# Placing VectorE's products of x with sine and cosine where GpSimd is planned idle, with narrower filler matmuls and a newly searched order

## The chip, the cores and the metric

One core of one Trainium2 chip. The metric is the device time of one execution in microseconds. Each run also has a span (first to last instruction, some 1.8 us less than the time) and a mean granted TensorE clock, 1.00 being full speed. A run is called slow here when it is over 1.5% above the fastest run of its own kernel, otherwise fast.

## The reference

Two stages follow each other. The first is a linear attention with a decaying state, over 4 batches, 8 heads, 768 steps and head size 48. The second works on its output x of 4 x 768 x 384:

```python
theta = x @ w_theta
zr, zi = x * cos(theta), x * sin(theta)
y = einsum('ts,bsd->btd', w_tok_r, zr) + einsum('ts,bsd->btd', w_tok_i, zi)
u = x + y
return u + maximum(u @ w_ch, 0)
```

## The kernel before

The kernel cuts the sequence into 24 chunks of 128 steps. For each it records operations (an engine, a modelled duration, dependencies, buffers). A list scheduler in the kernel's own text then simulates the engines and puts all operations into one order, and they are issued in that order. Semaphores between engines follow only from data and buffers. This is the part that places one operation (`free_at` holds the planned end of each engine's last one):

```python
    def place(self, o, free_at):
        ...                                   # cut: buffers
        for i, (eng, dur, fn, pen) in enumerate(o.alts):
            t = max(free_at.get(eng, 0.0), t_slot)
            for d in o.deps:
                t = max(t, d.end + (LAG[d.eng] if d.eng != eng else 0.0))
            ...                               # cut: loads
            out.append((t + dur + pen, t, eng, dur, i))
        return out
```

Tables named SHIFT, PENALTY, SLACK and WIN bias that order. They were found by a search. Copies have alternatives on two engines (`alts`), and the planner picks one, so other tables also move copies between VectorE and ScalarE. The operations that the change is about, `z`, are the products of x with sine and cosine:

```python
    def phases(g, ahead):
        deps = [st[g[-1]]["o_xc"]]
        ...
        toS = P.op("ACT", 1.3, lambda: table("trig_and_small"), deps, mode="toS", ...)
        ...                                   # cut: theta on TensorE, then:
            o_s = P.op("ACT", ACT(384), f_s, [o_th, toS], [], [], mode="S", ...)   # sine
            o_c = P.op("ACT", 0.46, f_c, [o_s], [], [th], mode="S", ...)           # cosine
            def f_z(b=b, c=c, sc=sc):
                xb = x_all[:, b, c:c + 1, :].to_broadcast([L, 2, DM])
                nc.vector.tensor_tensor(get(zb[b])[:, c], xb, get(sc), op=ALU.mult)
            s["o_z"] = P.op("DVE", 0.69, f_z, [o_c, z_open[b]], ...)
        if g[-1] < NT - 1:
            P.op("ACT", 1.3, lambda: table("natural_log_exp_and_others"), cs, mode="toE", ...)
```

Filler matmuls on zeros were put in to keep TensorE's clock up; what this case shows of that is in e13 and e14 (with few of their columns three of six runs had a mean clock of 0.956, with more none was under 0.966). FLEAD = 33 of them stand ahead of everything, and later ones go into planned gaps, as many as the last 3.4 us of the plan lack of a target in columns. Each is counted as 128 columns:

```python
    wps = pads["cum"][0][:, 1, DM:]
    def fill():
        nc.tensor.matmul(wps, lhsT=warm[:, 0, :], rhs=warm[:, 1, :], start=True, stop=True)
```

## Time and profile before

| kernel before | |
|---|---|
| time, median of 3 runs (range) | 170.01 us (168.47 to 171.23) |
| span and clock of the profiled run | 168.1 us, 0.984 |
| TensorE without useful work (idle + fillers) | 25.7 of 168.1 us |
| useful TensorE time | 142.4 us |

"Useful" is the span less idle time and fillers. The prediction works this out by stretches.

From the page of the kernel before: each engine's busy time, share and instructions, and the granted clock in tenths over 40 equal slices of 4.2 us.

```profile
PE 153.9 (92%) x1986; PEld 103.7 (62%) x1986; DVE 132.3 (79%) x287; ACT 116.0 (69%) x264; POOL 112.4 (67%) x133
PEclk9959999999999999999999999999999999999997
```

TensorE is nearly always busy. The clock is at its top but for one slice, the third (and the very end). The first 5 us of the kernel before, the busy time of TensorE in the filler matmuls alone (columns: stretch, length, TensorE busy and count, weight loads, clock, DMA share, GB/s):

```profile
0.00:5.00 5.00, 3.88 (x36) 3.75 (x36) 1.00 0.56 137
```

Thirty-six fillers of 128 columns, 3.88 us, cover the time until the first input has come. At some 108 ns each they run at half the rate of later ones (four matmuls of as many columns later take 0.22 us, start to start), so the 1.00 that is printed for the clock before the first real work is not to be trusted. The lengths of single matmuls show when the half rate ends: at about 5.6 us here, 4.3 us in the changed kernel. Below this is called the first rise.

### The profile page before, as it was taken

To read this page: it belongs to the slowest core of one execution; us is meant where nothing else is said; L and a number is where in the kernel's file an instruction comes from. 1 tells how busy PE (TensorE), PEld (TensorE's weight loads), DVE (VectorE), ACT (ScalarE), POOL (GpSimd) and SP (SyncE) were. 2 spreads that over 40 slices of the span, in tenths; PEclk is the share of its full clock that TensorE was granted. 3 is DMA by queue.
4 is the path that set the end of the run, shared out by engine and by line. 5 is a ranking of instruction groups with operands and counts; after the bars stand their busy time and mean duration, and the time that the engine had idled before them with its cause. 6 is when DMAs were issued, how large, how long until landed. Compare 5 with 4: busy or idle time off the path is not lost.

```text
span 168.1 us, 5063 instructions
## 1 busy us (share of the span) xinstructions
PE 153.9 (92%) x1986; PEld 103.7 (62%) x1986; DVE 132.3 (79%) x287; ACT 116.0 (69%) x264; POOL 112.4 (67%) x133
## 2 busy tenths in 40 slices
PE   7997798995898999999999999999899999999981
PEld 7575476763665676657566677666566666666640
DVE  4506958899999988797899998899988997436361
ACT  3556585699889997667998696489979963932000
POOL 7198488997986689866367989999979921000000
PEclk9959999999999999999999999999999999999997
DMA  4999999897989999999999999897911101020312
GB/s 102 277 261 248 252 258 177 161 285 174 272 227 215 268 244 281 258 284 216 207 188 206 251 179 221 168 223 142 236 41 47 49 4 66 30 97 0 140 47 94
DMA packets 93769, 29.81 MB, mean 177 GB/s; under 512 B 88369, under 2 KB 92210, under 8 KB 93746
## 3 DMA queue, kind: packets, MB, share of 16 engines
q1 hardware_dynamic: 93344, 29.50, 79.2%
q8 instruction: 15, 0.25, 0.6%
q14 instruction: 8, 0.07, 0.2%
q10 hardware_dynamic: 402, 0.00, 0.1%
HBM read 24.78 MB, written 4.72 MB: 175 GB/s over the span
## 4 chain that ended last, share of the span: by engine, by line
PE 71%; DVE 11%; ACT 8%; POOL 3%; DMA 2%; issue 2%; ACTq 0%; POOLq 0%
PE bank L978 25%; PE bank L1005 7%; PE bank L941 4%; DVE sb_z L955 4%; PE cum L1073 3%; PE bank L611 3%; PE bank L548 3%; PE bank L992 2%; DMA in_w<-in_w_dram 2%; PE bank L606 2%; PE bank L530 2%; PE bank L532 2%; PE bank L632 2%; PE bank L1054 2%; PE cum L435 2%
## 5 line engine op out<-in xcount | busy, mean ns | idle before, releaser
L978 PE MATMUL bank<-sb_z,wtokT 128*128 128x384 bf16 x288 | 53.8, 326 | 0.0
L978 PEld LDWEIGHTS <-wtokT 128*128 128x128 bf16 x288 | 26.0, 98 | 14.9
L524 POOL TENSOR_TENSOR sb_bon<-sb_v,sb_rub 128x384 bf16<-128x384 bf16 x18 | 14.9, 829 | 13.5 <-DVE sb_rub L520 5.5
L955 DVE TENSOR_TENSOR sb_z<-x_all,sb_sc 128x768 bf16<-128x768 bf16 x24 | 20.2, 858 | 1.6 <-ACT sb_sc L949 1.6
L463 POOL TENSOR_TENSOR sb_q<-in_r,sb_a 128x384 bf16<-128x384 f32 x18 | 18.6, 1035 | 2.8 <-ACT sb_alt L449 2.4
L457 POOL TENSOR_TENSOR sb_k<-in_k,sb_a 128x384 bf16<-128x384 f32 x18 | 18.6, 1032 | 1.4 <-DMA in_k<-in_k_dram 1.4
L508 POOL TENSOR_TENSOR sb_ru<-in_r,u_bc 128x384 f32<-128x384 f32 x18 | 19.2, 1069 | 0.2
L987 DVE TENSOR_TENSOR sb_un<-bank,x_all 128x384 bf16<-128x384 f32 x24 | 13.3, 554 | 7.6 <-PE bank L978 7.3
L444 ACT ACTIVATE sb_a<-cum 128x768 f32<-128x768 f32 x18 | 14.8, 824 | 4.2 <-PE cum L439 2.7
L515 POOL TENSOR_TENSOR sb_ruk<-sb_ru,in_k 128x384 bf16<-128x384 f32 x16 | 17.2, 1075 | 0.5
L327 ACT ACT_TABLE_LOAD x12 | 15.4, 1283 | 1.5 <-PEq L1089 1.3
L1005 PE MATMUL bank<-wch,sb_uT 128*128 128x384 bf16 x72 | 15.5, 327 | 0.6 <-DVE sb_uT L999 0.5
L1010 DVE SCALAR_TENSOR_TENSOR sb_o<-bank,sb_un 128x384 f32<-128x384 f32 x24 | 13.2, 553 | 3.6 <-PE bank L1005 3.3
L1073 PE MATMUL cum<-warm 128*128 128x128 bf16 x106 | 11.6, 262 | 4.4 <-ACT sb_rub L783 1.8
L949 ACT ACTIVATE sb_sc<-bank,hpi 128x384 bf16<-128x384 f32 x24 | 14.7, 612 | 0.0
L941 PE MATMUL bank<-wth,sb_xT 128*128 128x384 bf16 x72 | 14.0, 326 | 0.3 <-ACT sb_sc L949 0.3
L536 DVE COPY sb_qkt<-bank 128x1024 bf16<-128x1024 bf16 x18 | 12.3, 684 | 1.6 <-PE bank L532 1.5
L946 ACT ACTIVATE sb_sc<-bank 128x384 bf16<-128x384 f32 x24 | 12.4, 516 | 1.4 <-PE bank L941 1.3
L996 ACT ACTIVATE sb_uT<-bank 128x384 bf16<-128x384 bf16 x14 | 7.0, 503 | 9.0 <-PE bank L992 8.9
L636 ACT ACTIVATE sb_xT<-bank 128x384 bf16<-128x384 bf16 x15 | 7.3, 496 | 8.3 <-PE bank L632 8.3
L553 DVE TENSOR_TENSOR sb_p<-bank,mask_exc 128x512 bf16<-128x512 f32 x18 | 12.3, 683 | 0.6 <-PE bank L548 0.5
L594 ACT ACTIVATE sb_S<-bank,sb_alt 128x48 bf16<-128x48 f32 x52 | 11.6, 323 | 1.7 <-PE bank L584 1.7
(135 smaller groups left out, 341.4 us busy)
## 6 DMA issues: line engine op xcount, KB each, us to landing
out_dram<-sb_o SPq DMA_DIRECT2D x24, 192.0 KB, 2.6
in_w<-in_w_dram SPq DMA_DIRECT2D x18, 192.0 KB, 4.9
in_r<-in_r_dram SPq DMA_DIRECT2D x18, 192.0 KB, 4.8
in_k<-in_k_dram SPq DMA_DIRECT2D x18, 192.0 KB, 4.5
in_v<-in_v_dram SPq DMA_DIRECT2D x18, 192.0 KB, 4.5
sb_w<-in_moe_w_tok_r_dram SPq DMA_DIRECT2D x6, 384.0 KB, 4.9
sb_w<-in_moe_w_tok_i_dram SPq DMA_DIRECT2D x6, 384.0 KB, 5.2
in_w<-in_w_dram SPq DMA_DIRECT2D x3, 384.0 KB, 5.0
```

Source lines behind the costliest of these rows:

```text
L327: nc.scalar.preload_act_table_set(name)
L444: nc.scalar.activation(get(a), get(cum)[:, :, :DM], AF.Exp)
L457: nc.gpsimd.tensor_tensor(get(kk)[:, :, :D], s["x_k"](), av(1), op=ALU.mult)
L463: nc.gpsimd.tensor_tensor(get(q)[:, :, :D], s["x_r"](), av(0), op=ALU.mult)
L508: nc.gpsimd.tensor_tensor(get(ru), s["x_r"](), u_bc, op=ALU.mult)
L515: nc.gpsimd.tensor_tensor(get(ruk), get(ru), s["x_k"](), op=ALU.mult)
L524: nc.gpsimd.tensor_tensor(get(bon), get(vb), get(rub).to_broadcast([L, H, D]), op=ALU.mult)
L941: nc.tensor.matmul(get(th), lhsT=get(s["xT"])[:, j, :], rhs=wth[:, j, :], start=(j == 0), stop=(j == NJ - 1))
L955: nc.vector.tensor_tensor(get(zb[b])[:, c], xb, get(sc), op=ALU.mult)
L978: nc.tensor.matmul(get(ac), lhsT=wtokT[:, q_, s_, ti, :], rhs=get(zb[b])[:, s_, q_, :], start=(s_ == 0 and q_ == 0), stop=(s_ == NCH - 1 a ...
L1005: nc.tensor.matmul(get(ml), lhsT=get(uT)[:, j, :], rhs=wch[:, j, :], start=(j == 0), stop=(j == NJ - 1))
L1073: nc.tensor.matmul(wps, lhsT=warm[:, 0, :], rhs=warm[:, 1, :], start=True, stop=True)
```

## The change

Intent: let the planner place each multiplication where VectorE and GpSimd are both free, because in the trace each takes longer beside the other (a multiplication took 0.56 us at 82.22 us, with GpSimd idle, and 1.20 at 83.68, with GpSimd at work, and GpSimd's next operation took 1.31 in place of 1.00); let it block GpSimd in the plan as well; and search the order anew with that. Nothing on the chip enforces the lock. With it come a dependency between table loads on ScalarE, which the planner needs to find an order at all, and fillers of 112 columns, clear of columns in which other results lie (H is 8). The planner still counts each filler as 128 columns.

```diff
+        self.lock = None
@@ place
             t = max(free_at.get(eng, 0.0), t_slot)
+            if o.lock:
+                t = max(t, free_at.get(o.lock, 0.0) - 0.02)
@@ order
                 free_at[eng] = o.end
+                if o.lock:
+                    free_at[o.lock] = max(free_at.get(o.lock, 0.0), o.end)
@@ the tables of the search (cut: two long lines)
-    SLACK = (3.98, 6.1)
+    SLACK = (3.34, 6.38)
-    WIN = {'PE': 0.1, 'ACT': 0.11, 'DVE': 0.16, 'POOL': 0.39, 'SP': 0.1}
+    WIN = {'PE': 0.0, 'ACT': 0.0, 'DVE': 0.11, 'POOL': 0.12, 'SP': 0.69}
@@ phases
+    modes = [None]
-        deps = [st[g[-1]]["o_xc"]]
+        deps = [st[g[-1]]["o_xc"], modes[-1]]
-            s["o_z"] = P.op("DVE", 0.69, f_z, ...)
+            s["o_z"] = P.op("DVE", 0.47, f_z, ...)
+            s["o_z"].lock = "POOL"
-            P.op("ACT", 1.3, lambda: table("natural_log_exp_and_others"), ...)
+            modes.append(P.op("ACT", 1.3, lambda: table("natural_log_exp_and_others"), ...))
@@ fillers
-    wps = pads["cum"][0][:, 1, DM:]
+    wps = pads["cum"][0][:, 1, DM + 2 * H:]
-        nc.tensor.matmul(wps, lhsT=warm[:, 0, :], rhs=warm[:, 1, :], start=True, stop=True)
+        nc.tensor.matmul(wps, lhsT=warm[:, 0, :], rhs=warm[:, 1, :L - 2 * H], start=True, stop=True)
```

More of the change, by code (lines that the diff above doesn't have):

```diff
@@ L212 @@
     OFF = {'ln': -2.2, 'cum': -2.1, 'exp': -2.05, 'alt': -2.04, 'q': -1.5, 'k': -1.45, 'v': -1.2, 'ru': -1.3, 'ruk': -1.2, 'rub': -1.2, 'bon': -1.1, 'tqk': -0.9, 'qkt': -0.9, 'p': -0.8, 'm0': -0.7, 'pc': -0.7, 'sel': -1.6, 'y': -0.5, 'x': -0.5, 'xt': -0.4, 'xc': -0.4, 'rk': -1.3, 'rkt': -1.2, 'rkc': -1.2, 'beta': -1.15}
-    SHIFT = {'M': -0.23, 'M@0': 3.78, 'M@1': -8.79, 'M@3': 4.37, 'Mp@0': 5.06, 'S': -3.32, 'S@0': 0.3, 'S@1': 4.4, 'S@3': -1.39, 'Sp@0': -0.82, 'alt': -2.71, 'alt@0': -6.46, 'alt@1': -5.24, 'alt@3': -1.0, 'bc@0': 2.73, 'beta@0': 6.96, 'bon': -7.28, 'bon@0': -11.25, 'bon@1': -1.68, 'bon@3': -15.43, 'cos': -4.6, 'cos@0': -8.64, 'cos@1': -3.05, 'cos@3': -4.08, 'cum': 2.98, 'cum@0': -0.21, 'cum@1': -0.34, 'cum@3': 0.03, 'cumo@0': -2.52, 'cump@0': 0.81, 'cwch': 2.19, 'cwch@1': 0.17, 'cwt': -0.63, 'cwt@1': -5.35, 'cwth': 0.26, 'cwth@1': -10.14, 'exk@0': 3.3, 'exp': -7.56, 'exp@0': -8.69, 'exp@1': -7.51, 'exp@3': -3.91, 'exq@0': -3.62, 'fin': 10.83, 'fin@0': 10.28, 'fin@1': 11.48, 'fin@3': 1.68, 'k': -2.66, 'k@0': -9.79, 'k@1': -1.84, 'k@3': 3.21, 'ldk': -0.07, 'ldk@0': 0.25, 'ldk@1': 0.18, 'ldk@3': -0.13, 'ldkp@0': -0.23, 'ldr': -0.52, 'ldr@0': -1.79, 'ldr@1': -1.7, 'ldr@3': -1.11, 'ldrp@0': -0.32, 'ldv': 0.27, 'ldv@0': 0.93, 'ldv@1': 0.57, 'ldv@3': 1.39, 'ldvp@0': 0.18, 'ldw': -1.63, 'ldw@0': -1.67, 'ldw@1': -2.55, 'ldw@3': -1.18, 'ldwp@0': -6.51, 'ln': -1.02, 'ln@0': 5.4, 'ln@1': -2.53, 'ln@3': 2.0, 'm': 1.57, 'm@0': 15.82, 'm@1': 14.98, 'm@3': 17.21, 'ml': 3.16, 'ml@0': -6.88, 'ml@1': -11.74, 'ml@3': -9.39, 'p': 4.22, 'p@0': 8.66, 'p@1': 17.51, 'p@3': 5.23, 'pc': 1.07, 'pc@0': 1.12, 'pc@1': -0.89, 'pc@3': -3.49, 'pp@0': -0.08, 'q': -0.33, 'q@0': -1.43, 'q@1': -1.77, 'q@3': 2.32, 'qkt': 1.93, 'qkt@0': 3.15, 'qkt@1': -5.42, 'qkt@3': -1.23, 'qktp@0': -4.05, 'rk@0': 4.47, 'rkc@0': 2.84, 'rkt@0': -3.15, 'ru': -2.75, 'ru@1': 3.2, 'ru@3': 4.03, 'rub': 1.54, 'rub@1': 3.87, 'rub@3': 6.62, 'ruk': -0.11, 'ruk@1': 4.75, 'ruk@3': 0.58, 'sel': 1.06, 'sel@0': 2.59, 'sel@1': 1.72, 'sel@3': -2.89, 'sin': 1.45, 'sin@0': 7.58, 'sin@1': 1.41, 'sin@3': 6.75, 'st': 0.43, 'st@0': -2.07, 'st@1': 5.27, 'st@3': -5.11, 'th': -5.14, 'th@0': -13.68, 'th@1': -11.99, 'th@3': -7.44, 'toE': -2.74, 'toE@0': 1.79, 'toE@1': 3.28, 'toE@3': 5.51, 'toS': -2.78, 'toS@0': 4.03, 'toS@1': 1.52, 'toS@3': 0.01, 'tok': -3.84, 'tok@0': -14.49, 'tok@1': -16.93, 'tok@3': -11.95, 'tqk': -0.37, 'tqk@0': -7.47, 'tqk@1': -3.98, 'tqk@3': -6.14, 'ubc': 3.86, 'ubc@1': -1.26, 'ublk@1': 12.81, 'ubm': 3.03, 'ubm@1': -0.13, 'uc': -4.81, 'uc@0': -0.8, 'uc@1': 1.76, 'uc@3': 5.44, 'un': 2.42, 'un@0': 3.41, 'un@1': 1.64, 'un@3': 0.26, 'ut': -3.32, 'ut@0': -11.88, 'ut@1': -17.65, 'ut@3': -16.65, 'v': 1.33, 'v@0': 1.16, 'v@1': 4.38, 'v@3': 2.97, 'wch': -0.56, 'wch@1': 4.47, 'wev': 2.67, 'wev@1': 3.64, 'wt': 0.86, 'wt@1': 1.37, 'wth': 0.4, 'wth@1': 0.12, 'wtr': 0.92, 'wtr@1': 4.43, 'x': 1.16, 'x@0': -4.58, 'x@1': -2.03, 'x@3': 1.47, 'xc': 1.62, 'xc@0': 0.36, 'xc@1': 6.08, 'xc@3': 2.79, 'xp@0': -4.33, 'xt': 0.48, 'xt@0': -1.77, 'xt@1': 4.35, 'xt@3': 2.35, 'y': -0.38, 'y@0': -2.78, 'y@1': 3.73, 'y@3': 5.0, 'yp@0': -0.46, 'z': -1.82, 'z@0': -4.98, 'z@1': -4.18, 'z@3': -2.79}
@@ L214 @@
-    PENALTY = {'S': 1.09, 'S@0': 1.12, 'S@1': -0.94, 'S@3': -3.96, 'bc@0': -0.71, 'bon@0': 2.38, 'cwch': -1.71, 'cwch@1': 2.81, 'cwt': 1.34, 'cwt@1': 3.16, 'cwth': 1.85, 'cwth@1': 0.93, 'k': 9.17, 'k@0': 10.47, 'k@1': 3.58, 'k@3': 6.59, 'pc': -1.22, 'pc@0': -2.79, 'pc@1': -4.91, 'pc@3': -5.2, 'qkt': 3.99, 'qkt@0': -0.11, 'qkt@1': 0.97, 'qkt@3': 1.62, 'qktp@0': 2.76, 'rk@0': 7.24, 'rkc@0': 3.74, 'ruk': -1.87, 'ruk@1': -0.54, 'ruk@3': -9.82, 'uc': 1.64, 'uc@0': -1.68, 'uc@1': 4.04, 'uc@3': -0.06, 'wev': -0.04, 'wev@1': -7.81, 'xc': -0.05, 'xc@0': -0.64, 'xc@1': 0.26, 'xc@3': 1.02, 'xp@0': 0.98}
+    SHIFT = {'M': -0.23, 'M@0': 3.78, 'M@1': -6.18, 'M@3': 6.62, 'Mp@0': 5.26, 'S': -3.32, 'S@0': 0.3, 'S@1': 6.59, 'S@3': 0.68, 'Sp@0': -0.68, 'alt': -2.71, 'alt@0': -7.92, 'alt@1': -3.85, 'alt@3': -3.16, 'bc@0': -2.41, 'beta@0': 8.1, 'bon': -7.28, 'bon@0': -11.68, 'bon@1': -4.82, 'bon@3': -16.83, 'cos': -4.6, 'cos@0': -10.9, 'cos@1': -3.18, 'cos@3': -6.72, 'cum': 2.98, 'cum@0': -0.21, 'cum@1': 0.55, 'cum@3': -3.61, 'cumo@0': -6.13, 'cump@0': 4.02, 'cwch': 2.19, 'cwch@1': -2.53, 'cwt': -0.63, 'cwt@1': -6.25, 'cwth': 0.26, 'cwth@1': -3.54, 'exk@0': 1.95, 'exp': -7.56, 'exp@0': -5.95, 'exp@1': -4.97, 'exp@3': -0.07, 'exq@0': -3.13, 'fin': 10.83, 'fin@0': 12.97, 'fin@1': 11.66, 'fin@3': 3.4, 'k': -2.66, 'k@0': -7.6, 'k@1': 3.92, 'k@3': 11.07, 'ldk': -0.07, 'ldk@0': 0.25, 'ldk@1': -0.41, 'ldk@3': -0.17, 'ldkp@0': 0.02, 'ldr': -0.52, 'ldr@0': -1.79, 'ldr@1': -1.92, 'ldr@3': -1.62, 'ldrp@0': -1.21, 'ldv': 0.27, 'ldv@0': 0.93, 'ldv@1': 0.19, 'ldv@3': 0.69, 'ldvp@0': 0.15, 'ldw': -1.63, 'ldw@0': -1.67, 'ldw@1': -2.09, 'ldw@3': -1.86, 'ldwp@0': -4.07, 'ln': -1.02, 'ln@0': 13.94, 'ln@1': 0.95, 'ln@3': 9.2, 'm': 1.57, 'm@0': 26.09, 'm@1': 23.77, 'm@3': 24.65, 'ml': 3.16, 'ml@0': -5.56, 'ml@1': -18.97, 'ml@3': -9.64, 'p': 4.22, 'p@0': 8.66, 'p@1': 14.97, 'p@3': 0.71, 'pc': 1.07, 'pc@0': 1.12, 'pc@1': -6.99, 'pc@3': -11.04, 'pp@0': -2.44, 'q': -0.33, 'q@0': -3.18, 'q@1': -3.3, 'q@3': -1.47, 'qkt': 1.93, 'qkt@0': 4.65, 'qkt@1': -1.14, 'qkt@3': -1.9, 'qktp@0': -2.73, 'rk@0': 3.64, 'rkc@0': 3.56, 'rkt@0': -3.48, 'ru': -2.75, 'ru@1': 3.01, 'ru@3': 2.84, 'rub': 1.54, 'rub@1': -1.69, 'rub@3': 6.59, 'ruk': -0.11, 'ruk@1': 3.88, 'ruk@3': 1.59, 'sel': 1.06, 'sel@0': 2.59, 'sel@1': -2.83, 'sel@3': -9.19, 'sin': 1.45, 'sin@0': 11.07, 'sin@1': 5.13, 'sin@3': 7.53, 'st': 0.43, 'st@0': -3.02, 'st@1': 2.87, 'st@3': -6.8, 'th': -5.14, 'th@0': -15.65, 'th@1': -4.15, 'th@3': -0.69, 'toE': -2.74, 'toE@0': -0.85, 'toE@1': -2.88, 'toE@3': 3.35, 'toS': -2.78, 'toS@0': 4.63, 'toS@1': 0.91, 'toS@3': 3.99, 'tok': -3.84, 'tok@0': -15.93, 'tok@1': -19.8, 'tok@3': -14.21, 'tqk': -0.37, 'tqk@0': -5.52, 'tqk@1': 1.97, 'tqk@3': -1.93, 'ubc': 3.86, 'ubc@1': -2.95, 'ublk@1': 19.95, 'ubm': 3.03, 'ubm@1': -2.04, 'uc': -4.81, 'uc@0': -6.32, 'uc@1': -4.14, 'uc@3': 1.48, 'un': 2.42, 'un@0': -1.4, 'un@1': -6.49, 'un@3': -9.41, 'ut': -3.32, 'ut@0': -10.56, 'ut@1': -21.29, 'ut@3': -18.71, 'v': 1.33, 'v@0': 4.75, 'v@1': 9.96, 'v@3': 8.06, 'wch': -0.56, 'wch@1': 4.81, 'wev': 2.67, 'wev@1': 3.84, 'wt': 0.86, 'wt@1': 1.04, 'wth': 0.4, 'wth@1': 0.61, 'wtr': 0.92, 'wtr@1': 6.87, 'x': 1.16, 'x@0': -4.58, 'x@1': -1.52, 'x@3': -1.66, 'xc': 1.62, 'xc@0': 4.23, 'xc@1': 7.28, 'xc@3': 6.11, 'xp@0': -7.19, 'xt': 0.48, 'xt@0': -10.11, 'xt@1': -2.37, 'xt@3': -3.74, 'y': -0.38, 'y@0': -2.78, 'y@1': 6.77, 'y@3': 10.43, 'yp@0': 0.4, 'z': -1.82, 'z@0': -5.82, 'z@1': -2.75, 'z@3': -3.52}
@@ new lines @@
+    PENALTY = {'S': 1.09, 'S@0': 1.12, 'S@1': -0.45, 'S@3': -2.12, 'bc@0': -0.34, 'bon@0': 0.28, 'cwch': -1.71, 'cwch@1': 3.73, 'cwt': 1.34, 'cwt@1': 1.4, 'cwth': 1.85, 'cwth@1': 1.11, 'k': 9.17, 'k@0': 12.79, 'k@1': 4.43, 'k@3': 8.94, 'pc': -1.22, 'pc@0': -2.79, 'pc@1': -2.21, 'pc@3': -2.5, 'qkt': 3.99, 'qkt@0': 2.63, 'qkt@1': 4.71, 'qkt@3': 4.28, 'qktp@0': 1.95, 'rk@0': 7.66, 'rkc@0': 1.91, 'ruk': -1.87, 'ruk@1': -1.25, 'ruk@3': -9.61, 'uc': 1.64, 'uc@0': -4.19, 'uc@1': 0.18, 'uc@3': -2.45, 'wev': -0.04, 'wev@1': -8.08, 'xc': -0.05, 'xc@0': -1.73, 'xc@1': -2.21, 'xc@3': 0.74, 'xp@0': -0.63}
@@ L955, in f_z @@
                 nc.vector.tensor_tensor(get(zb[b])[:, c], xb, get(sc), op=ALU.mult)
-            s["o_z"] = P.op("DVE", 0.69, f_z, [o_c, z_open[b]], [] if z_open[b] else [zb[b]], [sc], prio=g[-1] - 0.3, name=f"z{n}")
+            s["o_z"] = P.op("DVE", 0.47, f_z, [o_c, z_open[b]], [] if z_open[b] else [zb[b]], [sc], prio=g[-1] - 0.3, name=f"z{n}")
+            s["o_z"].lock = "POOL"
             z_open[b] = z_open[b] or s["o_z"]
@@ L959, in phases @@
         if g[-1] < NT - 1:
-            P.op("ACT", 1.3, lambda: table("natural_log_exp_and_others"), cs, mode="toE", prio=g[-1] - 0.3, name=f"toE{g[-1]}")
+            modes.append(P.op("ACT", 1.3, lambda: table("natural_log_exp_and_others"), cs, mode="toE", prio=g[-1] - 0.3, name=f"toE{g[-1]}"))
     def mixing(b, ti):
```

## The prediction

> **What bounds the kernel now.** I read four views of the kernel before, in this order: the engines' totals on the page, the busy time of every engine by stretch, the same table for the filler matmuls alone, and the order in time of VectorE and GpSimd around some of the multiplications that the change is about.
>
> The page's first part says that TensorE is busy for 92% of the span, VectorE for 79%, ScalarE 69%, GpSimd 67%. Averages over stages mislead, so the stretches come next. Columns: the stretch and its length, then busy us and instruction count of each engine, the granted clock, the DMA share and GB/s.
>
> ```profile
> 5.00:35.00 30.00, 26.11 (x488) 18.61 (x486) 19.52 (x48) 19.96 (x48) 22.78 (x26) 0.94 1.10 233
> 35.00:60.00 25.00, 21.05 (x319) 15.03 (x316) 24.21 (x46) 23.37 (x49) 20.52 (x21) 1.00 1.04 243
> 60.00:163.00 103.00, 102.01 (x1153) 65.89 (x1148) 85.03 (x169) 71.09 (x168) 65.35 (x68) 1.00 0.70 152
> ```
>
> From 60 to 163 us TensorE (first pair) is idle for only 103.00 - 102.01 = 1.0 us, so nothing that another engine saves there can shorten the span. From 35 to 60 us VectorE (third pair) is busy 24.21 of 25 us and ScalarE 23.37, while TensorE has idle time. TensorE's busy time also holds filler matmuls on zeros[...] (line 1073):
>
> ```profile
> 5.00:35.00 30.00, 5.13 (x52) 3.92 (x50) 0.94 1.10 233
> 35.00:60.00 25.00, 2.54 (x23) 1.50 (x20) 1.00 1.04 243
> ```
>
> TensorE's time without useful work is then: 5.0 us of start; 30.00 - 26.11 + 5.13 = 9.0 us up to 35 us; 25.00 - 21.05 + 2.54 = 6.5 us from 35 to 60; 1.0 us up to 163; and about 4.2 us of tail (0.89 busy of the last 5.10). Together 25.7 us; the other 142.4 of 168.1 us are useful TensorE work. The changed kernel must do the same useful work: the listing of its instructions differs on TensorE in fillers and order alone. So the change can only win from these 25.7 us, and really only from the 9.0 and the 6.5.
>
> The multiplication of x by sine and cosine is line 955, on VectorE, 24 times:
>
> ```profile
> L955 DVE TENSOR_TENSOR sb_z<-x_all,sb_sc 128x768 bf16<-128x768 bf16 x24 | 20.2, 858 | 1.6 <-ACT sb_sc L949 1.6
> L955 DVE TENSOR_TENSOR sb_z<-x_all,sb_sc x24: 543/840/1396, 38.1 to 148.6; 128x768 bf16<-128x768 bf16 x24
> ```
>
> One shape, yet 543 ns at the fastest, 840 at the median, 1396 at worst. The reason can be read off 82 to 86 us, VectorE first, then GpSimd (start, duration):
>
> ```profile
> 82.22 0.56 DVE L955 TENSOR_TENSOR sb_z<-x_all,sb_sc 128x768 bf16<-128x768 bf16 x1 [0.29 <-ACT sb_sc L949]
> 83.68 1.20 DVE L955 TENSOR_TENSOR sb_z<-x_all,sb_sc 128x768 bf16<-128x768 bf16 x1 [0.30 <-ACT sb_sc L949]
> ```
>
> ```profile
> 82.67 0.83 POOL L524 TENSOR_TENSOR sb_bon<-sb_v,sb_rub 128x384 bf16<-128x384 bf16 x1 [2.57 <-ACT sb_v L470]
> 83.46 1.00 POOL L515 TENSOR_TENSOR sb_ruk<-sb_ru,in_k 128x384 bf16<-128x384 f32 x1
> 84.41 1.31 POOL L457 TENSOR_TENSOR sb_k<-in_k,sb_a 128x384 bf16<-128x384 f32 x1
> ```
>
> At 82.22 GpSimd had nothing to do and the multiplication took 0.56 us. At 83.68 GpSimd was inside line 515 until 84.46; the multiplication ended at 84.88, some 0.42 us after it, and the next GpSimd operation took 1.31 us in place of 1.00. The two engines take turns, and both pay.
>
> [...]768 columns in 543 ns from SBUF, 384 in 554 ns from PSUM (line 987). [...]the granted clock is 1.00 everywhere from 15 us to 160 us.
>
> **The change, part by part.** The order is made by a list scheduler in the kernel's own text, with a modelled duration per operation; the changed tables are the outcome of a new search with it.
>
> 1. The multiplication is modelled at 0.47 in place of 0.69 us, may not start before GpSimd's running operation ends, and then holds GpSimd. No semaphore enforces it on the chip: only the order changes. In the trace the fast multiplication at 51.33 us gives way to the next VectorE instruction at 51.80, so 0.47 is its true step. Contention today costs VectorE 24 x (858 - 550) ns = 7.4 us, and GpSimd about 3.6 us (its four kinds of 1.00 us operation average 1.03 to 1.08). With real durations straying from the plan by a tenth or two, a multiplication that comes late meets the next GpSimd operation and waits a whole one. I therefore assume that only half is won: a mean of 0.70 us (estimate), 24 x 0.16 = 3.8 us of VectorE. Of these only the six between 35 and 60 us count (6.63 us busy today): 6.63 - 6 x 0.70 = 2.4 us.
> 2. Moved copies. The listing of instructions has six casts of x (548 ns) going from VectorE to ScalarE, ten copies to xT and seven to uT going from ScalarE (500 ns) to VectorE (350 ns), one copy of qkt (1.02 us) and two small ones also to VectorE, and one ruk product from VectorE (0.84) to GpSimd (1.07). Sum for VectorE: -7.2 if no multiplication waited at all, or -3.8 by my assumption, -3.3 + 3.5 + 2.5 + 1.1 + 0.4 - 0.8 = about -0.4 us; ScalarE: +3.1 - 5.0 - 3.5 - 1.0 - 0.4 = -6.8 us. But most xT and uT copies lie after 60 us, where TensorE sets the pace. In 35 to 60 us two casts (1.01 us together) leave VectorE for ScalarE. VectorE's load there falls by 2.4 + 1.0 = 3.4 us, to about 20.8 of 25; ScalarE's rises by 1.0 to 24.4 of 25 and takes its place. I take half of the 3.4, 1.7 us, as what TensorE gets back out of its 6.5.
> 3. Up to 35 us: the first twenty microseconds keep nearly the same order in the listing, and no engine is full (VectorE 19.52 of 30, GpSimd 22.78); this is latency of chains. Four casts leave VectorE. I allow 0.3 us.
> 4. Fillers: 113 of 112 columns in place of 106 of 128, and clear of the columns where beta lies. Waits of fillers for ScalarE's small copy sum to 1.8 us over five times before, but the listing still has a wait on fillers in ten places. I count nothing.
> 5. 60 to 163 us and the tail: useful work is the same, and both orders end alike (one last token product, then transpose, channel product, addition, store). Nothing.
>
> Sum: 1.7 + 0.3 = 2.0 us off the span of 168.1; off the time of 170.0 that gives 168.0.
>
> **The rivals.** (a) The lock is only on paper: order and jitter leave the multiplications at about 0.85 us, GpSimd's timetable slips by its reserved 24 x 0.47 = 11.3 us, and nothing is gained. For: [...]no semaphore between the two, and GpSimd is full in the stretch before 35 us. Against: GpSimd has nothing to do for over a quarter of the span. Time 169.5 to 170.5. (b) The early stage gets much better: with VectorE relieved, the token products (line 978), the large reserve of TensorE work, open earlier. For: in the new listing the first of them stands after about 29 us of useful TensorE work, in the old after about 32 ([...]an estimate from the listing and 0.162 us for 384 columns in the chain). Then half of the 15.5 us could shrink by a third: 165 to 166. Against: the new listing has more fillers before that point (109 against 106), a sign that the planner still expects gaps there. (c) VectorE becomes the bound between 60 and 140 us, where it is already at 85 to 97% and now gets seventeen more copies; if the multiplications still wait, TensorE loses 1 to 2 us: 170 to 171.5.
>
> **Range and chances.** The middle is 168.0. Rival (b) sets the low end at 165.4, (a) and (c) the high end at 170.3; the three runs of before lay between 168.47 and 171.23, which alone asks for some width. Faster by over 2% means below 166.6, which needs 3.4 us out of the 15.5: 0.27. Slower by over 2% needs a broken middle stage: 0.05. Within 2%: 0.68.
>
> **What would show it right or wrong.** Step 1: line 955's mean, 0.70 us if right, near 0.86 if rival (a); GpSimd's 1.00 us operations nearer 1.00. Step 2: VectorE below 22 us busy in 35 to 60, ScalarE above 24, TensorE's time without useful work there at about 4.8 us. Step 3: that time up to 35 us still near 9. Step 5: TensorE idle by no more than 1 to 1.5 us from 60 us to its last stretch, useful work 142 us. I am wrong if the early time without useful work stays at 15.5 us, or falls below 12, or if the middle stretch opens gaps.

## The result, and the profile after

The changed kernel takes 175.04 us (median of 4 runs, 174.94 to 175.45), the kernel before 170.56 us in the same rounds (4 runs, 168.47 to 171.23). A ratio in this text is the mean time of one kernel's fast runs over that of the other's fast runs of the same rounds, so not quite the ratio of the medians. Here it is 1.035 [1.026, 1.043]: slower, and outside the predicted range. All four runs have a clock of 0.955 to 0.957. The profiled one has a span of 173.1 us.

From the page of the changed kernel: engines, granted clock, and the group of the multiplications (after the bar: busy us and mean ns; then the idle time before them and what ended it).

```profile
PE 156.6 (90%) x1993; PEld 105.5 (61%) x1993; DVE 132.4 (77%) x300; ACT 110.2 (64%) x250; POOL 111.9 (65%) x134
...
PEclk9855599999999999999999999999999999999998
...
L962 DVE TENSOR_TENSOR sb_z<-x_all,sb_sc 128x768 bf16<-128x768 bf16 x24 | 18.3, 780 | 2.5 <-ACT sb_sc L956 2.3
```

The multiplications did become shorter, 780 instead of 858 ns in the mean. But the clock row has three slices at 5 where it had one. The same table by stretches that the prediction showed of before, now of the changed kernel (busy time and count of TensorE, weight loads, VectorE, ScalarE, GpSimd, then clock, DMA share, GB/s):

```profile
5.00:35.00 30.00, 25.37 (x392) 17.38 (x392) 16.33 (x40) 17.64 (x44) 19.11 (x22) 0.77 1.11 240
35.00:60.00 25.00, 20.70 (x337) 14.49 (x338) 19.99 (x38) 22.26 (x47) 21.67 (x23) 1.00 0.96 207
60.00:163.00 103.00, 101.23 (x1198) 67.02 (x1199) 89.84 (x191) 68.76 (x160) 67.35 (x70) 1.00 0.71 155
```

And its fillers alone:

```profile
5.00:35.00 30.00, 5.09 (x52) 4.12 (x52) 0.77 1.11 240
35.00:60.00 25.00, 2.05 (x25) 1.46 (x25) 1.00 0.96 207
```

TensorE's time without useful work follows as in the prediction (the stretch less busy plus fillers, for instance 30.00 - 25.37 + 5.09 = 9.7), for both kernels and for two experiments that come later:

| us without useful work | to 5 | 5-35 | 35-60 | 60-163 | tail | sum | useful |
|---|---|---|---|---|---|---|---|
| before (span 168.1) | 5.0 | 9.0 | 6.5 | 1.0 | 4.2 | 25.7 | 142.4 |
| after (173.1) | 5.0 | 9.7 | 6.35 | 1.8 | 4.2 | 27.1 | 146.0 |
| e15 (170.5) | 5.0 | 9.8 | 6.7 | 1.8 | 4.2 | 27.5 | 143.0 |
| e17 (169.5) | 5.0 | 9.9 | 5.5 | 2.9 | 4.2 | 27.5 | 142.0 |

The span grew by 5.0 us: 3.6 us because the same useful work took longer, and 1.4 us because TensorE stood idle or on fillers for longer. These are two separate causes, and the experiments treat them so.

**The clock.** Stretches of half a microsecond show where it falls. Before (TensorE busy, clock, DMA share, GB/s):

```profile
9.00:9.50 0.50, 0.50 (x8) 0.50 1.28 260
...
12.50:13.00 0.50, 0.50 (x4) 1.00 1.44 289
```

After:

```profile
7.50:8.00 0.50, 0.50 (x2) 0.72 1.26 262
...
21.00:21.50 0.50, 0.50 (x2) 0.63 1.13 272
```

In tenths of a microsecond the clock is 0.50 up to 21.3 us and 1.00 from 21.4, so a mean of 0.63 in half a microsecond is 0.37 us at half and 0.13 at full speed. Half speed then holds from 9.0 to 12.4 us before, from 7.7 to 21.4 us after: 3.4 and 13.7 us, the second four times the first. Counted in the same way, in part from means over 16 to 30 us and then good to some 0.3 us, the half-speed stretches in the 20 profiles, after the first rise and up to the tail, are 3.4 to 3.6 us long (before, e6, e8, e13, e15, e16, e18), 6.6 to 6.8 (e9, and a second one in e3 and in e13), 13.6 to 13.8 (after, e3, e5, e14) and 24.0 (e2); the other seven profiles have none. No run here tests what sets these lengths. TensorE was not idle meanwhile: in the changed kernel it was busy for 3.44 of the 4 us from 5 to 9 us and for 11.10 of the 12 us from 9 to 21. What the fillers did just before, in the changed kernel's first 5 us, and then the order in time on TensorE there (start, duration, in brackets the idle time before it and what ended it; the view begins inside the fillers and shows the last 29 of the 36):

```profile
0.00:5.00 5.00, 3.44 (x36) 3.28 (x36) 1.00 0.60 137
```

```profile
1.75 2.81 PE L1081 MATMUL cum<-warm 128*128 128x112 bf16 x29
5.29 0.74 PE L696 MATMUL bank<-sb_lw,pm_in 128*128 128x384 bf16 x2 [0.74 <-ACT sb_lw L676]
```

The first real matmul starts at 5.29 us as it did before (5.32), because it waits for ScalarE and the input. But the narrower fillers are done sooner, and TensorE stands for 0.74 us where it stood for 0.18. Whether that gap is what lets the clock fall is taken up under e13 and e14.

**The order.** The gap that opened after 60 us stands near 122 us. VectorE in the changed kernel:

```profile
121.91 3.13 DVE L962 TENSOR_TENSOR sb_z<-x_all,sb_sc 128x768 bf16<-128x768 bf16 x3
124.97 0.68 DVE L541 COPY sb_qkt<-bank 128x1024 bf16<-128x1024 bf16 x1
```

GpSimd at the same time, then TensorE:

```profile
122.05 1.31 POOL L462 TENSOR_TENSOR sb_k<-in_k,sb_a 128x384 bf16<-128x384 f32 x1
123.32 1.31 POOL L520 TENSOR_TENSOR sb_ruk<-sb_ru,in_k 128x384 bf16<-128x384 f32 x1
```

```profile
125.70 0.24 PE L584 MATMUL bank<-sb_S,ident 128*128 128x192 bf16 x1 [0.95 <-DVE sb_qkt L541]
```

The planner put three multiplications behind each other where GpSimd was to be idle. On the chip GpSimd was at work then (which of the two had slipped is not shown): 3.13 us for three, each GpSimd operation at 1.31 instead of 1.00, and the copy of qkt behind them kept TensorE waiting for 0.95 us. In the plan this cannot happen; without a semaphore it does.

### The profile page after: what moved, and what is told of

It is laid out like the page before. It is cut to its first block, busy times and chain, and to the rows that moved or that the text cites.

```text
span 173.1 us, 5074 instructions
## 1 busy us (share of the span) xinstructions
PE 156.6 (90%) x1993; PEld 105.5 (61%) x1993; DVE 132.4 (77%) x300; ACT 110.2 (64%) x250; POOL 111.9 (65%) x134
## 4 chain that ended last, share of the span: by engine, by line
PE 66%; DVE 16%; ACT 10%; DMA 2%; issue 2%; POOL 2%; ACTq 0%; POOLq 0%
PE bank L986 25%; PE bank L1013 6%; DVE sb_z L962 6%; PE bank L616 3%; PE bank L948 3%; PE cum L1081 2%; PE bank L1000 2%; DMA in_w<-in_w_dram 2%; PE bank L553 2%; PE cum L696 2%; PE bank L611 2%; DVE sb_qkt L541 2%; PE cum L440 2%; PE bank L637 2%; PE bank L535 2%
## 5 line engine op out<-in xcount | busy, mean ns | idle before, releaser
L529 POOL TENSOR_TENSOR sb_bon<-sb_v,sb_rub 128x384 bf16<-128x384 bf16 x18 | 15.9, 886 | 8.1 <-DVE sb_rub L525 7.0
L962 DVE TENSOR_TENSOR sb_z<-x_all,sb_sc 128x768 bf16<-128x768 bf16 x24 | 18.3, 780 | 2.5 <-ACT sb_sc L956 2.3
L513 POOL TENSOR_TENSOR sb_ru<-in_r,u_bc 128x384 f32<-128x384 f32 x18 | 17.9, 998 | 0.1
L1081 PE MATMUL cum<-warm 128*128 128x112 bf16 x113 | 10.6, 253 | 5.3 <-DVE warm L301 1.1
L953 ACT ACTIVATE sb_sc<-bank 128x384 bf16<-128x384 f32 x24 | 12.4, 515 | 3.2 <-PE bank L948 3.2
L809 DVE COPY sb_qkt<-bank 128x1024 bf16<-128x1024 bf16 x6 | 6.0, 995 | 9.6 <-PE bank L820 6.0
L541 DVE COPY sb_qkt<-bank 128x1024 bf16<-128x1024 bf16 x18 | 12.3, 683 | 0.5 <-PE bank L537 0.4
L525 DVE TENSOR_REDUCE sb_rub<-sb_ruk 128x8 f32<-128x384 bf16 x18 | 9.7, 541 | 3.5 <-POOL sb_ruk L520 3.5
L1081 PEld LDWEIGHTS <-warm 128*128 128x128 bf16 x113 | 8.9, 120 | 5.7 <-issue 4.4
```

Source lines behind the costliest of these rows:

```text
L513: nc.gpsimd.tensor_tensor(get(ru), s["x_r"](), u_bc, op=ALU.mult)
L529: nc.gpsimd.tensor_tensor(get(bon), get(vb), get(rub).to_broadcast([L, H, D]), op=ALU.mult)
L541: nc.vector.tensor_copy(get(qkt), get(tp))
L1081: nc.tensor.matmul(wps, lhsT=warm[:, 0, :], rhs=warm[:, 1, :L - 2 * H], start=True, stop=True)
```

## The experiments

Eighteen kernels ran. The kernel before ran 110 times beside them. Where an experiment concerns the clock, the clock of every run is what counts.

### e1 and e6: the changed kernel with wide fillers

```diff
-    wps = pads["cum"][0][:, 1, DM + 2 * H:]
+    wps = pads["cum"][0][:, 1, DM:]
-... rhs=warm[:, 1, :L - 2 * H] ...
+... rhs=warm[:, 1, :] ...
```

> The changed kernel, order and lock untouched, with the filler matmuls back at 128 columns (113 of them, and over the columns of beta again). Theory A (the narrower fillers let the granted TensorE clock stay at half speed from 7.7 to 21.2 us in place of 9.0 to 12.3): mean clock back to about 0.98, clock at half for under 5 us, useful TensorE busy time from 146.0 back to about 142.4 us, time 170.5 to 172, so 3 us or more faster than the changed kernel. Rival B (the new order is the cause, the clock is a bystander): clock may change, time stays at 174 to 175.5.

> The changed kernel with fillers of 128 columns, once more, beside the run before it. Theory A: most runs at a clock of 0.985 or more and 171.4 to 172.0 us, one in four at most at 0.965. Rival B: the same mixture of clocks as in the changed kernel. Either way the best runs stay above 171 us, since the new order costs about 1.9 us at full clock.

e1: 171.45, 171.94, 171.90 us at clocks of 0.988 to 1.0 and one slow run of 175.78 at 0.965. Ratio 1.012 [1.009, 1.016]. e6, on another chip: median 172.5, ratio 1.010 [1.006, 1.015], clocks 0.966 to 0.998. Width alone brings back some 3 us. What remains near full clock, about 2 us, is the order. e1's profile has 27.4 us without useful work against 25.7, so 1.7 of the 2 us, and 142.2 us useful.

### e2: the kernel before with narrow fillers

```diff
-    wps = pads["cum"][0][:, 1, DM:]
+    wps = pads["cum"][0][:, 1, DM + 2 * H:]
-... rhs=warm[:, 1, :] ...
+... rhs=warm[:, 1, :L - 2 * H] ...
```

> The kernel before, order untouched, with fillers of 112 columns as in the change. Theory A: mean clock falls to about 0.955, half speed for some 13 us early, time 173 to 174.5, 2% over before. Rival B: time within 0.5% of before, 169.5 to 171.

Three fast runs at 169.55 to 170.66 us, clocks 0.977 to 0.994, and one slow at 176.43 with 0.922, which was the profiled one: half clock from 8 to 32 us. Ratio 1.003 [0.998, 1.007]. So the old order was in the low state too with narrow fillers, but once in four runs (with wide ones, 1 of its 110 runs had a mean clock of 0.96 or less).

### e3: the changed kernel with 38 fillers at the start

```diff
-    FLEAD = 33
+    FLEAD = 38
```

> The changed kernel with 38 leading fillers in place of 33, each still 112 columns wide: the fillers in front cover the same 4600 columns and the same time up to about 5.1 us as before, those later stay narrow. If the gap in front of the first real matmul (0.74 us in the changed kernel, 0.18 before) is what lets the clock fall: clock about 0.975 to 0.985, time 171 to 172.5. If it is the later, narrower fillers: clock still about 0.956, time about 175. Rival B: 174 to 175.5 whatever the clock.

Clocks of 0.956, 0.956, 0.942 and once 0.998; times 175.08, 175.00, 179.67 and 172.81 us. Ratio 1.026 [1.019, 1.034]. A miss for the idea that the five more at the start are enough. Its slow run was the profiled one, and showed something else that comes back below.

### e5: the changed kernel again, unchanged, on the chip of e6

> The changed kernel once more, unchanged, on the same chip as the next run, to see how often its clock stays low. Theory A (narrow fillers let the clock fall for long): most runs at a mean clock near 0.956 and at 174.5 to 175.5 us, as in 4 of 4 runs so far. Rival B (which clock a run gets is chance): clocks spread as in the run with wide fillers, about half at 0.98 or more, these at 171 to 173 us.

174.91 and 174.97 us at 0.955 and 0.956, but also 172.49 at 0.985, 182.09 at 0.921, and 176.91 and 177.86 at 0.977 and 0.975. Ratio 1.027 [1.021, 1.033]. The low clock is a frequent state, not the only one.

### e13 and e14: is it the width of a filler or the columns in all?

e13 keeps 112 columns but counts them as 112 and starts with 38: 131 fillers, 14,700 columns. e14 has 128 columns but counts them as 146 and starts with 29: 97 fillers, 12,400 columns. The changed kernel has 113 and 12,700.

```diff
@@ e13, in the issue loop, and FLEAD
-                    past.append((o.start, 128 * n))
+                    past.append((o.start, 112 * n))
@@ e14
+                    past.append((o.start, 146 * n))
@@ both: the same factor in every place where 128 columns or their duration are counted
```

> The changed kernel with its narrow fillers of 112 columns, but counted as 112 by the planner and with 38 instead of 33 of them at the start: 131 fillers and 14,700 filler columns in place of 113 and 12,700. Same order of everything else. If the amount of filler work is what the clock reacts to (theory A), the granted clock goes to 0.98 or above in most of the six runs and the time to about 172. If the single filler's width, or the phase in which the work falls, is what counts (theory B), most runs stay at 0.955 to 0.98 and the time near 175. The run with 38 at the start alone stayed at 0.956 in two of four.

> The changed kernel with fillers of 128 columns again, but fewer of them (97, 29 of them at the start, some 12,400 filler columns, about as many as the 12,700 of the changed kernel). Theory A (amount): the clock falls to 0.955 to 0.98 in most runs, time 174 to 176. Theory B (width or phase): the clock stays at 0.98 or above in most runs, time about 172, as with 113 wide ones.

The two pages' clock rows, e13 first, then e14:

```profile
PEclk9969999999858999999999999999999999999998
```

```profile
PEclk9855599999999999999999999999999999999998
```

e14 repeats the changed kernel's row and time, with wide fillers: 174.91, 174.96 and 175.04 us at 0.956 (and 172.96, 176.08, 176.15 at 0.996 to 0.999); median 175.0, ratio 1.026 [1.019, 1.033]. e13 has no run at 0.956: 170.31, 170.79, 171.6 at 0.987 to 0.999, others at 172.94, 176.48 and 177.67; median 172.27, ratio 1.006 [1.000, 1.011]. So it is the amount of filler work, not the width of one filler: theory A, on both sides.

All profiles can now be sorted by the columns that fillers streamed in the first 5 us. The changed kernel and e5 have 36 x 112 = 4,032, e2 the same, e14 31 x 128 = 3,968, e3 38 x 112 = 4,256: all five show half clock from about 8 us for 13.6 us or more. The fifteen others (before, and e1, e4, e6 to e13, e15 to e18) have 41 x 112 = 4,592 or 36 x 128 = 4,608: after its first rise none is at half clock for more than 3.6 us before 21 us. I found this border after the fact, and it is the border of this kernel's start, not a rule. The total of filler columns sorts the same way (12,880 or fewer in the five, 13,568 or more in the others), and no run varies the start alone across the border. But the fall at 7.5 to 8.0 us comes before all later fillers: in the five, none runs between the start and the fall.

Neither the gap before the first real matmul nor the moment of the first rise explains it alone. In the five the gap is 0.73 to 0.93 us and the first rise comes at 4.1 to 4.6 us. In e6, e11, e12 and e17, with wide fillers, the gap is 0.42 to 0.85 us and the rise comes at 3.8 to 4.6; e6 then falls for 3.5 us, the other three not at all.

One thing the clock row hides. In e7 and e10 (profiled runs of 170.07 and 172.64 us) it shows 9 up to the tail, yet TensorE ran at half rate from the start to 13.4 and 14.0 us: the clock was late to rise for the first time, and the time before the first rise is printed as 1.00. The same 18 fillers in e10, then in e11:

```profile
9.77 2.10 PE L1091 MATMUL bank<-warm 128*128 128x128 bf16 x18
```

```profile
8.28 1.18 PE L1091 MATMUL bank<-warm 128*128 128x128 bf16 x18
```

A mean clock does not see this either. The kernel before has 31 runs at 0.991 to 0.995: 9 take 168.1 to 168.8 us, 22 take 171.0 to 171.8, and none lies between. A late first rise would look like that; none of these runs has a profile, so it is not shown.

By single runs, with that blind spot: a mean clock of 0.96 or less is in 14 of 24 runs of the five kernels with few columns, in 2 of 126 runs of the other experiments, and in 1 of 110 of the kernel before.

### e4 and e8: the lock without its tables

e4 is the kernel before with the lock, 0.47 us and the dependency of table loads, with the old tables. e8 has the dependency alone, as a control.

```diff
@@ both
-        deps = [st[g[-1]]["o_xc"]]
+        deps = [st[g[-1]]["o_xc"], modes[-1]]
@@ e4 only
+            s["o_z"].lock = "POOL"      # and 0.69 -> 0.47, place() and order() as in the change
```

> The kernel before with its old search tables and wide fillers, but with the lock, the 0.47 us and the dependence of each table load on the one before (without that dependence the planner finds no order). The lock alone, without the new search. If the lock works as meant, the multiplications' mean falls from 858 to about 700 to 780 ns; time 168 to 172, since TensorE sets the pace and the tables were searched for another model. If the lock itself is harmful (GpSimd's timetable slips): over 172.

> A control for the run with the lock on the old tables: the kernel before with only the dependence of each table load on the one before, no lock, old duration. The order shifts a little without any lock. If the 2.4% of the lock run came from the lock: this one stays within 0.5% of before (169 to 171). If any replanning of searched tables costs that much: 172 to 174, and the lock run says nothing of the lock itself.

e4: 174.54 us, ratio 1.024 [1.017, 1.031], at a clock of 0.99 to 1.0. The multiplications take 710 ns in the mean, yet TensorE has 6.4 us without useful work from 60 to 163 us, against 1.0. e8: 169.52 us, 0.999 [0.995, 1.003]. So the dependency costs nothing, and the lock with the shorter duration (the two were not tried apart) makes multiplications shorter and the order worse, with tables that were searched for another model. With the new search and wide fillers (e1, 1.012) half of that loss is left.

### e7 and e9: early fillers in a PSUM bank of their own

The first 57 fillers write to a bank that nothing else needs then, so they wait for no small copy of ScalarE (1.8 us over five times in the kernel before). e7 is that on the kernel before, e9 on e1. (With 58 the kernel deadlocks; the build finds that.)

```diff
+    early = pps.tile([L, 512], f32, tag="bank5", name="bank5")
+    count = [0]
     def fill():
+        count[0] += 1
+        dst = early[:, :L] if count[0] <= 57 else wps
```

> The kernel before with only this changed: its first 57 filler matmuls write into a PSUM bank that nothing uses yet, so that they no longer wait for ScalarE to have read the running sums (0.5 us at 8.2 us, 0.9 us at 13.4 us in the trace of before). If waiting fillers are what lets the clock fall from 9.0 to 12.3 us: clock 0.99 to 1.00, the third exponential at about 17.5 us in place of 19.0, time 168.3 to 169.3, 0.5 to 0.9% faster. If the clock there is chance: within 0.3% of before.

> The changed order with fillers of 128 columns of which the first 57 write into an unused PSUM bank (the edit that made the kernel before faster in 4 of 6 runs). Base for the next three. If what remains of the loss is the order: 170 to 171.5 with clocks of 0.985 to 1.00, so 1.5 to 2.5 us above the kernel before with the same edit (168.1 to 168.5 in its better runs).

e7: median 168.36, ratio 0.996 [0.991, 1.000], the best median, and not clear of noise. Its profiled run, 170.07 us, had the late first rise; four others took 168.1 to 168.5. e9: 172.48, ratio 1.014 [1.009, 1.019], no better than e1. So a gain from the fillers' waits is possible in the old order, not shown, and none is seen in the changed one.

### e10, e11, e12: two faults of the changed order moved out of the way

In e1 two copies of weights stand on ScalarE between the table load and the first sine. ScalarE in order of time, the kernel before first, then e1:

```profile
34.34 1.28 ACT L327 ACT_TABLE_LOAD   x1
35.63 0.49 ACT L766 ACTIVATE sb_rkT<-bank 128x384 bf16<-128x384 bf16 x1
36.09 0.49 ACT L946 ACTIVATE sb_sc<-bank 128x384 bf16<-128x384 f32 x1
```

```profile
35.65 1.28 ACT L332 ACT_TABLE_LOAD   x1
36.94 0.84 ACT L398 ACTIVATE sb_wn<-sb_w 128x768 bf16<-128x768 f32 x1
37.69 0.51 ACT L475 ACTIVATE sb_v<-in_v 128x384 bf16<-128x384 f32 x1
38.10 0.83 ACT L398 ACTIVATE sb_wn<-sb_w 128x768 bf16<-128x768 f32 x1
38.84 0.47 ACT L953 ACTIVATE sb_sc<-bank 128x384 bf16<-128x384 f32 x1
```

The table load itself is 1.3 us later (casts of x now stand before it), and the first sine 2.75 us. e10 puts the two weight copies behind the first sines; e11 puts the qkt copy of the gap near 122 us ahead in the burst of multiplications; e12 does both. All are on e9.

```diff
+        todo = self.order(window)
+        for name, behind in [('cwt00', 'cos1'), ('cwt10', 'cwt00'), ('qkt20', 'z13')]:   # e12
+            o = next(x for x in todo if x.name == name)
+            todo.remove(o)
+            todo.insert(1 + next(i for i, x in enumerate(todo) if x.name == behind), o)
```

> As the base, with two of ScalarE's weight copies (0.75 us each) moved from before the first two sine and cosine pairs to behind them; nothing else is reordered. Theory C (ScalarE, not VectorE, is what holds the first token product now: in the run with wide fillers its first sine came at 38.8 us against 36.1 before): the first multiplication 1.5 us earlier, time 0.4 to 1.5 us under the base. Rival D (the early stage is held elsewhere): within 0.3 us of the base, the copies' users then late in their turn.

> As the base, with one VectorE copy of transposed q and k moved ahead of the burst of multiplications at 118 us behind which TensorE stood still for 0.94 us (three multiplications that took 3.13 us where three free ones take 1.4). Theory E (the blocked burst is what opens gaps in the middle stage): TensorE's idle time from 60 to 163 us down from 1.8 to 2.4 us to about 1.0 to 1.4, time 0.5 to 1.0 us under the base. Rival: the gap moves to what now comes later (the multiplications and the token products), time within 0.3 us.

> Both moves together on the base. If both theories hold: 168.5 to 169.5, within 0.5% of the kernel before, and the order's loss is explained by two places. If neither: 170 to 171.5.

Medians of all six runs: 171.66, 172.11 and 170.97, against 172.48 for e9. Ratios to before: 1.002 [0.996, 1.008], 1.006 [0.999, 1.013], 0.999 [0.995, 1.004]. The spread is wide (168.99 to 176.24), and the rule for slow runs leaves out three of six in each, so the ratios flatter them. At a printed clock of 1.0, e11 took 169.19 and e12 169.51, e1 171.45, but their first rise came at 4.2 and 3.8 us and e1's only at 6.3, so part of that is clock. Time without useful work from 60 to 163 us is 1.2 us in e11 and 1.6 in e12, against 1.8 in their base e9 (2.4 in e1). The moves do what they should in the traces; what they are worth is not shown. By the medians both together gain 1.5 us, but by the means of six runs e9 has 172.2, e10 171.7, e11 172.9 and e12 171.1 us, and chance alone gives such differences (for e9 and e12, in one of five random splits of their runs).

### e15: GpSimd waits for the first multiplication

The profiles of two slow runs, e3's and e13's, caught something that no other one shows. VectorE in e13, then GpSimd, then TensorE:

```profile
41.47 6.41 DVE L962 TENSOR_TENSOR sb_z<-x_all,sb_sc 128x768 bf16<-128x768 bf16 x1
```

```profile
41.87 0.85 POOL L529 TENSOR_TENSOR sb_bon<-sb_v,sb_rub 128x384 bf16<-128x384 bf16 x1
42.66 1.01 POOL L462 TENSOR_TENSOR sb_k<-in_k,sb_a 128x384 bf16<-128x384 f32 x1
...
46.46 1.01 POOL L520 TENSOR_TENSOR sb_ruk<-sb_ru,in_k 128x384 bf16<-128x384 f32 x1
```

```profile
48.54 0.48 PE L918 MATMUL bank<-ident,x_all 128*128 128x128 bf16 x3 [5.17 <-DVE sb_qkt L541]
```

One multiplication lasts 6.41 us. It begins while one GpSimd operation is running, six more then go ahead of it, back to back and none of them stretched, and it ends only when GpSimd has run out of work. TensorE stands for 5.17 us, and meanwhile, at 46.6 us, its clock falls again (the 858 in e13's row). In e3 the same multiplication, the first of all, also took 6.41 us. In the changed kernel's own profile it began at 44.44 us, also 0.40 us ahead of the same GpSimd operation and also inside the one before it, and the two took turns: 0.87 us, and 1.16 for GpSimd's. What decides between the two outcomes is open. e15 adds to e1 a copy of one column that reads the first multiplication's result on GpSimd, so that a semaphore holds GpSimd:

```diff
                 nc.vector.tensor_tensor(get(zb[b])[:, c], xb, get(sc), op=ALU.mult)
+                if not fenced:
+                    fenced.append(n)
+                    nc.gpsimd.tensor_copy(fence, get(zb[b])[:, c, 0, :1])
```

> The changed kernel with wide fillers (as in e1 and e6), and a copy of one column on GpSimd that reads the result of the first multiplication, so that GpSimd's next operations wait by semaphore for the end of that one multiplication. Theory: the slow runs above 175 us are those in which this first multiplication is blocked for 6.41 us while GpSimd runs on (seen in both profiles of slow runs that caught it, e3 and e13[...]). Then no run of six is over 174, no clock is at 0.965, and the fast ones stay at 171 to 172. Rival: the slow runs have another cause; then one or two of six are again over 175.

22 runs were taken: 169.59 to 173.39 us, median 172.25, clock 0.973 to 1.0, none over 174. The 59 runs of before beside it have a median of 170.18; the ratio is 1.007 [1.003, 1.011], from the 9 of 22 runs that the rule calls fast. The single cost of this fence is a copy of 188 ns. So the runs over 175 us are gone, and the ordinary ones are where e1's were: the order's 2 us stand. Over all kernels of the changed order with enough filler columns, runs over 175 us are 6 of 40 without a fence (e1, e6, e9 to e13) and 1 of 72 with one (e15 to e18), and that one has the low clock, 0.957. The limit of 175 was chosen after seeing the runs, and only two of the slow runs have a profile. No kernel without a fence ran on the chip of e15 in the same rounds. That the blocked multiplication makes most of them is therefore likely, and shown for two.

### e16, e17, e18: a real lock

e16 is e15 with the two moves of e12. e17 is e15 with the fence behind all 24 multiplications. e18 is e17 with the moves.

```diff
-                if not fenced:
+                if True:                # e17, e18
```

> As e15, and the two moves of e12 as well (two copies of weights behind the first sines, one qkt copy behind another multiplication), without the separate bank for early fillers. If the moves and the fence add up, six fast runs at 169 to 170.5, level with or just under the kernel before (170); if the moves were worth nothing, 171 to 172.

> As e15, but with such a fence behind each of the 24 multiplications: the planner's lock made real in one direction (GpSimd waits for the multiplication; the multiplication still may meet a running GpSimd operation). Theory A: contention falls further, mean of the multiplications 0.65 to 0.70 us, and the time is as e15 or up to 1 us less. Theory B: GpSimd now waits for the chain of ScalarE and VectorE, its products come late, and the time is 1 to 3 us longer than e15.

> All that helped the changed order together: wide fillers, the semaphore behind each of the 24 multiplications (e17) and the two moves (e16). If the two gains are independent (about 1 us each against e15), the median of all runs is 169.5 to 170.3, level with the kernel before or just under it. If the fence already frees what the moves freed, it is that of e17, 170.5 to 171.3.

e16: median 171.19 of 22 runs, ratio 1.006 [1.004, 1.009], not the 169 to 170.5 that was expected if the moves and the fence add up; by the means (171.5 against 171.9) its lead over e15 is within chance. e17: 170.97 of 22 runs, ratio 1.002 [1.000, 1.005]. e18: 172.16 of 6 runs, ratio 1.014 [1.009, 1.019]: a miss, the gains do not add up. The multiplications on e17's page, and its burst in the middle on VectorE:

```profile
L964 DVE TENSOR_TENSOR sb_z<-x_all,sb_sc 128x768 bf16<-128x768 bf16 x24 | 14.5, 620 | 3.2 <-ACT sb_sc L958 3.0
```

```profile
119.86 1.87 DVE L964 TENSOR_TENSOR sb_z<-x_all,sb_sc 128x768 bf16<-128x768 bf16 x3
```

Three multiplications now take 1.87 us, GpSimd's next two 1.00 each instead of 1.31, and the gap of 0.95 us on TensorE behind the burst is gone. Theory A of e17 holds: contention is nearly out (a mean of 620 ns against 788 in e15 and 543 at the fastest, with 24 copies on GpSimd of 258 ns in the mean), and the median is 1.3 us below e15 (1.1 us by the means, which chance gives in under one of 100 random splits). But the profiles do not show that gain as less lost time. Both have 27.5 us without useful work (the table above); the 1.0 us between their spans is useful time, at a clock of 0.989 in e15 and 0.995 in e17. What e17 wins from 35 to 60 us it loses after 60, and 1.05 us of that is one new wait on TensorE near 69 us, behind a copy of weights:

```profile
69.66 1.62 PE L1018 MATMUL bank<-wch,sb_uT 128*128 128x384 bf16 x9 [1.05 <-ACT wch L398]
```

Those weights came late from memory (ScalarE waited 1.81 us for their load). The same wait is in e16 and e18, 1.08 and 1.12 us, and not in e15. Why it comes with them, and why e18 stands behind both, I have not settled. No version of the changed order beats the kernel before.

## Why the prediction was wrong

It said 168.0 us, by winning 2.0 us; the kernel lost 4.5 (medians of the same rounds), and 5.0 between the profiled spans. By its own steps:

**Step 4, the fillers: "I count nothing".** This is the step that failed most. Its size is 3.6 us: the same useful work took 146.0 instead of 142.4 us, because half clock held for 13.7 instead of 3.4 us. The sentence before the steps, that the changed kernel must do the same useful work, was right as work and wrong as time. The prediction had the diff of the fillers in hand and quoted a clock of 1.00 from 15 us on; it did not ask what the clock does before 15 us with an eighth fewer columns at the start. e1, e13 and e14 show the cause: too few filler columns (the three fast runs of e1 had clocks of 0.988 to 1.0 and those of e13 of 0.987 to 0.999; e14 had 0.956 in three of six).

**Step 5, 60 to 163 us: "Nothing".** It failed by 0.8 us in the profile after (1.8 against 1.0), and by 1.4 in e1 at full clock. Rival (c) had the kind right, gaps in the middle stretch when multiplications still wait, and put it at 170 to 171.5 us. e1, with the clock out of the way, lies just above that.

**Step 2, 35 to 60 us: 1.7 us to win.** The cause happened, the gain did not. VectorE fell from 24.21 to 19.99 us, more than foreseen; ScalarE stayed at 22.26, under the 24 foreseen; TensorE's lost time went from 6.5 to 6.35 and not to 4.8. The step took half of VectorE's relief as TensorE's. But the longest wait of TensorE there is now one on ScalarE, for a copy of weights:

```profile
48.93 0.51 PE L1062 MATMUL bank<-ident,sb_wn 128*128 128x128 bf16 x6 [1.06 <-ACT sb_wn L398]
```

The same 1.06 us stand in e1, e16 and e17. The kernel before had 0.18 us on such a copy, and its longest wait there was 1.01 us on VectorE. The change also made the chain of table load, sine, cosine and multiplication begin later: the first sine went from 36.1 to 43.1 us (38.8 in e1). What that costs is not shown: in e16, which moves two copies behind it, it comes at 38.87 us against 40.33 in e15, and TensorE's lost time in this stretch is 6.5 against 6.7 us.

**Step 1, the mean of the multiplications.** 780 ns was measured; 700 was assumed, and 860 was rival (a). The direction was right (858 ns before), the size was half. In 35 to 60 us the six took 5.20 us where the step put 6 x 0.70 = 4.2. "A multiplication that comes late meets the next GpSimd operation and waits a whole one" is what the trace shows (1.20 us at 83.68 us in the kernel before), but its worst case was missing: waiting for seven, as in e3 and e13.

**Step 3, up to 35 us: 0.3 us to win.** 9.7 against 9.0, in the wrong direction. At full clock in e1 it is 9.6, so this is the order's, not the clock's.

**Rival (b)** was half right: the first token product came at 50.4 instead of 51.7 us (46.1 in e1), and it brought nothing, since the gaps stayed. Its 165 to 166 us also needs a third of half of 15.5, 2.6 us, on top of the 2.0 of the main line, which it does not say.

Sum: 3.6 us of clock and 1.4 us of order make the 5.0 us of span. The order alone, near full clock, is about 2 us (e1, e15). Still open: why a start with few filler columns goes low in 14 of 24 runs and not in all, what sets the lengths of the half-speed stretches, when the clock rises first, the spread of e15's ordinary runs between 170 and 173 us, and e18.

## What to carry to other kernels

Fillers are part of a change: here an eighth fewer of their columns at the start went with a larger loss (3.6 us of span) than the new order did (1.4). Count their columns ahead of the first real work, and compare useful time as well as idle time, because a lower clock looks like busy time (146.0 us of useful time at 0.956, 142.4 at 0.984). Check a printed clock against the length of a matmul that you know (1.00 stood here over fillers of 108 ns; four matmuls of as many columns later took 0.22 us). A lock in a planner is a wish until a semaphore carries it (three multiplications in a row took 3.13 us without one, 1.87 with it), and a tighter plan has more places where a small slip meets a busy neighbour; ask for the longest instance of a contended operation (6.41 us in e3 and e13), not only for its mean. Relief on an engine is worth something only if the wait that ends last stands on that engine (from 35 to 60 us VectorE was busy for 4.2 us less and TensorE won 0.15); list TensorE's waits in the stretch before turning saved VectorE time into saved TensorE time.
